# Splitting the first product of chunk 0, sharing the casts of row 1, and letting loads go by VectorE writes

## Chip, cores, metric

One core of a Trainium2 chip. The metric is the device time of one execution in microseconds (us), each kernel run several times. A run counts as slow when it is over 1.5% above the fastest run of the same kernel. That is a label by time alone and says nothing of the cause. Comparisons below use the other runs, called fast; where a median is over all runs, the text says so.

## The reference

Eight rows (batch) of attention with eight heads, 576 positions, head dimension 64. Four heads attend to the last 32 positions, four to every fourth of the last 128. The result, as 4608 tokens of 512 values, goes through a feed-forward layer with a squared relu.

```python
scores = scale * np.matmul(q, k.transpose(0, 1, 3, 2))
mask_plain = (rel >= 0) & (rel < 32)
mask_dil = (rel >= 0) & (rel < 128) & (rel % 4 == 0)
attn = softmax(np.where(masks, scores, -1e9))        # masks by head
x = np.matmul(attn, v).transpose(0, 2, 1, 3).reshape(4608, 512)
h = x @ w_in                 # 512 -> 2048
g = np.maximum(h, 0.0) ** 2
return g @ w_out             # 2048 -> 512
```

## The kernel before

The tokens are cut into nine chunks of 512. TensorE does the *first product* of a chunk (`ph`, with w_in), ScalarE the relu, VectorE the square, TensorE the *second product* (`po`, with w_out). The attention of row b+1 is woven into the products of chunk b. The order of instructions on each engine is the order in which the program writes them: `pump(n)` writes down n steps of the pending product, and what is written between two pumps lands between those steps.

Rows 0 and 1 come through on-chip casts and TensorE transposes. From row 2 on, q and k are copied to DRAM scratch as f16 (`dk`, four copies issued by GpSimd) and transposed by DMA into `QKTx` and `QKTd` (issued by SyncE).

```python
    def store(c, t, po, ots):                 # used by the second product of chunk 0
        ...
        nc.scalar.copy(ot[:, t % 2, :], po)
        if t % 2 == 1:
            rows = out[(c * 4 + t - 1) * P : (c * 4 + t + 1) * P, :]
            nc.gpsimd.dma_start(out=rows.rearrange("(t p) m -> p t m", p=P), in_=ot)

    def keep_qk(b):                           # dk: DRAM to DRAM, f32 to f16
        ...
        for lo in (0, half):
            for i, src in ((1, k), (0, q)):
                nc.gpsimd.dma_start(out=d[i, lo : lo + half], in_=...)
        return d
```

`hold` is a small tile that orders engines: VectorE writes it, then GpSimd does, so GpSimd goes on only once VectorE has come that far.

```python
    ... # row 0: scores and values
    load_sliding_qk(1); load_v(1); load_dilated_qk(1)
    cast_sliding_qk(1, (nc.gpsimd,) * 4)
    load_w_out()
    cast_sliding_v(nc.gpsimd, 2)
    cast_dilated_v(nc.gpsimd, 2)
    g0 = hidden(0)
    pending.append(mm1_gen(0, g0))            # first product of chunk 0
    pump(22)
    begin(1, lambda: pump(1))                 # row 1: transposes and scores
    pump(1000)
    pending.append(mm2_by_rows_gen(0, g0))    # second product; its stores as above
    pump(4)
    ...
    def rows_and_load():
        pump(2)
        n_val[0] += 1
        if n_val[0] == 2:
            nc.vector.memset(hold, 0.0)

    attn_values(1, rows_and_load, True)       # row 1: values
    nc.gpsimd.memset(hold, 0.0)
    dk = keep_qk(2)
    load_v(2)
    transpose_by_dma(dk)
    pump(1000)

    for b in range(2, B):
        pending.append(moe_gen(b - 1))
        ...
        if b == 2:
            ... # GpSimd copies one element of QKTx and QKTd to hold
            dk = keep_qk(b + 1)
            ...
            cast_v(nc.scalar)
            load_v(b + 1)
            pump(4)
        ...
        for g in range(2):
            s_sliding_x(b, g)                 # the scores `ps`, read QKTx
            pump(5)
```

The softmax here doesn't subtract the row's maximum and nothing guards it: scores larger than these inputs give would overflow.

## Time and profile before

| | before |
|---|---|
| time, median of 3 runs | 321.75 us (321.33 to 322.06) |
| span of the profiled run | 318.8 us |
| TensorE busy | 93% |
| mean granted TensorE clock | 0.994 |
| second product of chunk 0 ends (next first product starts) | 67.78 us |
| row 2's q and k transposed (QKTx landed) | 75.34 us |
| first scores of row 2 (ps) | 76.94 us |
| chunks 2 and 3 start | 100.81 and 133.54 us |

Points in time are from the start of the span. (Where the text below gives the end of the second product, it is the start of its last product, 0.2 us earlier: 67.57 here.)

### The profile page before, as it was taken

The page shows a single profiled execution, that of the slowest core. Times are in us where ns is not written, and L with a number is a line of the kernel's source. Part 1 is how long each engine was busy: PE and PEld are TensorE (multiplying, and loading weights), DVE is VectorE, ACT ScalarE, POOL GpSimd, SP SyncE. Part 2 cuts the span into 40 slices and gives each one's busy share as a digit, 9 for nine tenths or more (in the row PEclk, how much of TensorE's full clock was granted, in tenths as well). Part 3 has the DMA queues.
Part 4 walks back from the last instruction along what each step waited for, and adds up shares of the span by engine and source line. Part 5 has one row for each costly group of instructions (what it writes and reads, how often), then busy time and mean ns, then how long its engine had stood idle before and what let it go on. Part 6 is the DMA issues. An engine that isn't in the chain of part 4 may idle for free.

```text
span 318.8 us, 6927 instructions
## 1 busy us (share of the span) xinstructions
PE 295.8 (93%) x2876; PEld 192.5 (60%) x2876; DVE 207.4 (65%) x397; ACT 181.6 (57%) x310; POOL 48.3 (15%) x83
## 2 busy tenths in 40 slices
PE   6768888999998999999999999999999999999992
PEld 2665344544596458845884588458845884684582
DVE  5584486626976597659765976597659765824833
ACT  2754593268934983498349834983498236415620
POOL 4362490213103100120012001200100010000000
PEclk9999997999999999999999999999999999999999
DMA  8999999989998999099939992999220002003003
GB/s 182 236 182 236 209 202 207 238 206 224 211 198 210 204 211 198 23 253 213 191 48 266 201 187 53 251 213 189 53 111 0 2 28 106 0 2 132 2 0 132
DMA packets 82766, 47.88 MB, mean 150 GB/s; under 512 B 67760, under 2 KB 78512, under 8 KB 82352
## 3 DMA queue, kind: packets, MB, share of 16 engines
q1 hardware_dynamic: 74516, 25.99, 42.5%
q0 software_dynamic: 6848, 19.80, 28.0%
q10 hardware_dynamic: 1372, 1.67, 1.9%
q8 instruction: 22, 0.36, 0.5%
q14 instruction: 8, 0.07, 0.1%
HBM read 39.85 MB, written 16.52 MB: 177 GB/s over the span
## 4 chain that ended last, share of the span: by engine, by line
PE 64%; ACT 12%; DMA 11%; DVE 5%; SPq 3%; issue 3%; POOL 1%; ACTq 0%; DVEq 0%; POOLq 0%
PE ph L302 26%; PE poa L350 9%; PE pob L350 8%; PE poc L350 7%; PE pod L350 4%; DMA early<-in_q_dram 3%; ACT vd L145 3%; ACT vp L145 3%; DMA dk<-in_k_dram 3%; DMA QKTx<-dk 2%; DMA sv<-in_v_dram 2%; SPq L106 2%; PE pav L571 2%; PE paw L585 2%; ACT rt L290 2%
## 5 line engine op out<-in xcount | busy, mean ns | idle before, releaser
L302 PE MATMUL ph<-xT,wi 128*128 128x512 f16 x576 | 131.9, 380 | 2.3 <-ACT rt L290 1.7
L290 ACT ACTIVATE rt<-ph 128x512 f16<-128x512 f32 x144 | 83.7, 607 | 23.9 <-PE ph L302 19.7
L302 PEld LDWEIGHTS <-wi 128*128 128x128 f16 x576 | 54.1, 98 | 64.7 <-issue 4.6
L294 DVE TENSOR_TENSOR g<-rt 128x1024 f16<-128x1024 f16 x63 | 44.9, 713 | 50.8 <-ACT rt L290 50.5
L350 PEld LDWEIGHTS <-sm 128*128 128x128 f16 x512 | 47.1, 98 | 7.5 <-issue 2.6
L350 PEld LDWEIGHTS <-g 128*128 128x128 f16 x384 | 35.9, 98 | 6.4 <-DVE g L294 0.3
L350 PE MATMUL poa<-wo,g 128*128 128x256 f16 x256 | 32.8, 273 | 0.1
L350 PE MATMUL pob<-T,sm 128*128 128x256 f16 x256 | 32.5, 272 | 0.0
L606 ACT COPY xT<-px 128x576 f16<-128x576 f16 x16 | 10.2, 640 | 36.9 <-PE px L600 36.9
L366 POOL DMA_DIRECT2D out_dram<-otl x6 | 4.5, 757 | 162.2 <-DVE otl L396 142.8
L624 ACT COPY xT<-py 128x576 f16<-128x576 f16 x16 | 10.2, 638 | 23.0 <-PE py L618 23.0
L554 DVE TENSOR_TENSOR x_d<-paw,rcp_d 72x512 f16<-72x512 f32 x32 | 22.0, 686 | 1.1
L493 DVE TENSOR_TENSOR AT<-AT,maskp 128x576 f16<-128x576 f16 x32 | 16.7, 532 | 7.4 <-ACT AT L492 6.4
L492 ACT ACTIVATE AT<-pz 128x576 f16<-128x576 f32 x32 | 19.3, 680 | 2.6 <-PE pz L539 2.6
L492 ACT ACTIVATE AT<-ps 128x576 f16<-128x576 f32 x32 | 19.3, 664 | 0.4
L553 DVE RECIPROCAL rcp_d<-paw 72x8 f32<-72x8 f32 x32 | 6.5, 203 | 19.5 <-PE paw L585 19.4
L350 PE MATMUL poc<-T,sm 128*128 128x256 f16 x128 | 16.2, 272 | 2.1 <-ACT otu L385 2.1
L554 DVE TENSOR_TENSOR x_p<-pav,rcp_p 96x512 f16<-96x512 f32 x24 | 16.5, 687 | 0.8
L323 PE MATMUL po<-wo,g 128*128 128x512 f16 x64 | 16.9, 399 | 0.0
L350 PE MATMUL poc<-wo,sm 128*128 128x256 f16 x128 | 16.3, 273 | 0.0
L350 PE MATMUL pod<-T,g 128*128 128x256 f16 x128 | 16.1, 273 | 0.0
L493 DVE TENSOR_TENSOR AT<-AT,maskd 128x576 f16<-128x576 f16 x32 | 14.6, 495 | 1.7 <-ACT AT L492 1.5
(89 smaller groups left out, 327.4 us busy)
## 6 DMA issues: line engine op xcount, KB each, us to landing
sv<-in_v_dram SPq DMA_DIRECT2D x40, 128.0 KB, 9.8
sd<-in_v_dram SPq DMA_DIRECT2D x7, 512.0 KB, 6.6
dk<-in_k_dram POOLq DMA_DIRECT2D x12, 288.0 KB, 7.0
dk<-in_q_dram POOLq DMA_DIRECT2D x12, 288.0 KB, 8.7
out_dram<-otl POOLq DMA_DIRECT2D x6, 512.0 KB, 3.4
out_dram<-otu POOLq DMA_DIRECT2D x6, 512.0 KB, 4.3
wi<-in_moe_w_in_dram POOLq DMA_DIRECT2D x2, 1024.0 KB, 11.0
wo<-in_moe_w_out_dram POOLq DMA_DIRECT2D x4, 512.0 KB, 9.7
```

Of the source, the lines that this page charges most:

```text
L145: nc.scalar.copy(o, i)
L290: nc.scalar.activation(rt[:, o, :], ph[:], ACTF.Relu)
L294: nc.vector.tensor_mul(g[:, ffc - 1 : ffc + 1, :], rt, rt)
L302: nc.tensor.matmul(ph, wi[:, dmk, ffc * P : ffc * P + P], xs[:, dmk, :], start=(dmk == 0), stop=(dmk == NDM - 1),)
L323: nc.tensor.matmul(po, g[:, ffc, t * P : (t + 1) * P], wo[:, ffc, :], start=(ffc == 0), stop=(ffc == NFF - 1),)
L350: nc.tensor.matmul(acc[:, t, :], lhs[:, k, t * P : (t + 1) * P], rhs[:, k, :], start=(first and t == 0 and k == 0), stop=(k == NK - 1), sk ...
L492: nc.scalar.activation(AT[:, u, 0:UW], ps[:, :, 0 : UW // 2], ACTF.Exp, scale=scale)
L493: nc.vector.tensor_mul(AT[:, u, 0:UW], AT[:, u, 0:UW], mask)
L553: nc.vector.reciprocal(rcp[0:w], pv[:, :, :, D])
L554: nc.vector.tensor_tensor(out=x[0:w], in0=pv[:, :, :, 0:D], in1=rcp[0:w].unsqueeze(3).to_broadcast([w, 2, HH, D]), op=ALU.mult,)
L606: nc.scalar.copy(xT[:, 0:2, t0 : t0 + 288], px[:, 0:UW].rearrange("x (c t) -> x c t", c=2),)
L624: nc.scalar.copy(xT[:, 2:4, t0 : t0 + 288].rearrange("x c (i r) -> x c i r", r=DIL), py[:, 0:UW].rearrange("x (c r i) -> x c i r", c=2, r= ...
```

## The change

The intent is to start the first product earlier and to take away the waits of row 1. The first 288 tokens of chunk 0 get their own part of the first product, which starts while row 0's last values are still to come. Row 1's q and k casts go from GpSimd to ScalarE and VectorE, its v casts to ScalarE. The w_out load and row 2's v loads are each held until a VectorE write lets them go, so that they keep off the queues of earlier loads.

```diff
+    def mm1_part_gen(c, g, t0, t1):          # first product for tokens t0 to t1
+        ...
-    cast_sliding_v(nc.gpsimd, 2, 0, 2)
+    cast_dilated_v(nc.gpsimd, 2)
     load_w_in()
-    cast_sliding_v(nc.gpsimd, 2, 2, NB)
-    cast_dilated_v(nc.gpsimd, 2)
+    cast_sliding_v(nc.gpsimd, 2)
     ... (row 0; its last values now stand between pumps of the first part)
-    cast_sliding_qk(1, (nc.gpsimd,) * 4)
-    load_w_out()
-    cast_sliding_v(nc.gpsimd, 2)
-    cast_dilated_v(nc.gpsimd, 2)
-    pending.append(mm1_gen(0, g0))
-    pump(22)
-    begin(1, lambda: pump(1))
+    pending.append(mm1_part_gen(0, g0, 0, 288))
+    ...
+    pending.append(mm1_part_gen(0, g0, 288, TOKC))
+    pump(2)
+    nc.vector.memset(hold, 0.0)
+    nc.gpsimd.memset(hold, 0.0)
+    load_w_out()
+    pump(1)
+    cast_sliding_qk(1, (nc.scalar, nc.vector, nc.scalar, nc.vector))
+    pump(2)
+    transposes_and_scores(1, lambda: pump(1))
     pump(1000)
+    cast_v(nc.scalar)
     pending.append(mm2_by_rows_gen(0, g0))
-    pump(4)
+    pump(3)
+    scores_dilated(1, lambda: pump(3))
     ...
         if n_val[0] == 2:
             nc.vector.memset(hold, 0.0)
+            nc.vector.memset(sv[:, :, :, 0:1], 0.0)
+            nc.vector.memset(sd[:, :, :, 0:1], 0.0)
     attn_values(1, rows_and_load, True)
     nc.gpsimd.memset(hold, 0.0)
     dk = keep_qk(2)
     ...
-            pump(4)
+            pump(8)
```

The line `dk = keep_qk(2)` is not touched. But three times `pump(3)` write 9 steps of the second product (two products each) ahead of row 1's values, where `pump(4)` wrote 4. With the 20 steps among the values that makes 29 before `keep_qk(2)`, where there were 24, and a store of chunk 0 belongs to step 28.

More of the change, by code (lines that the diff above doesn't have):

```diff
@@ L294, in relu_squared @@
             nc.vector.tensor_mul(g[:, ffc - 1 : ffc + 1, :], rt, rt)
+    def mm1_part_gen(c, g, t0, t1):
+        xs = xT[:, :, c * TOKC + t0 : c * TOKC + t1]
+        rt = None
+        for ffc in range(NFF):
+            ph = pmool.tile([P, TOKC], FP32, name=f"ph{c}_{ffc}_{t0}", tag="pm")
+            for dmk in range(NDM):
+                nc.tensor.matmul(
+                    ph[:, 0 : t1 - t0],
+                    wi[:, dmk, ffc * P : ffc * P + P],
+                    xs[:, dmk, :],
+                    start=(dmk == 0),
+                    stop=(dmk == NDM - 1),
+                )
+            o = ffc % 2
+            if o == 0:
+                rt = osb.tile([P, 2, TOKC], FP16, name=f"rt{c}_{ffc}_{t0}", tag="rt")
+            nc.scalar.activation(rt[:, o, 0 : t1 - t0], ph[:, 0 : t1 - t0], ACTF.Relu)
+            if o == 1:
+                r = rt[:, :, 0 : t1 - t0]
+                nc.vector.tensor_mul(g[:, ffc - 1 : ffc + 1, t0:t1], r, r)
+            yield
     def mm1_gen(c, g, sm=None):
@@ L627, in x_dilated, with transposes_and_scores @@
         )
-    def begin(b, fill, wide=False):
+    def transposes_and_scores(b, fill):
         for hp in range(2):
             for i in (1, 0):
-                t_sliding(b, hp, i, wide)
+                t_sliding(b, hp, i)
                 fill()
@@ L637, in begin, with scores_dilated @@
             for i in (1, 0):
-                t_dilated(b, g, i, wide, eng=nc.scalar)
+                t_dilated(b, g, i, eng=nc.scalar)
                 fill()
+    def scores_dilated(b, fill):
         for g in range(2):
@@ L663, in attn_values @@
         x_dilated(b, 1, zs, wide)
+    hold = const.tile([P, 1], FP32, name="hold")
     cast_sliding_qk(0, (nc.scalar, nc.scalar, nc.vector, nc.gpsimd))
-    cast_sliding_v(nc.gpsimd, 2, 0, 2)
+    cast_dilated_v(nc.gpsimd, 2)
     load_w_in()
-    cast_sliding_v(nc.gpsimd, 2, 2, NB)
-    cast_dilated_v(nc.gpsimd, 2)
+    cast_sliding_v(nc.gpsimd, 2)
     pj = pmool.tile([P, TOKC], FP32, name="pj", tag="pm")
     idle_matmuls(pj, 14, TOKC)
-    n_idle = [0]
     def idle():
-        n_idle[0] += 1
         idle_matmuls(pj, 5, P)
-    begin(0, idle)
-    def idle_and_load():
-        idle()
-        if n_idle[0] == 15:
-            nc.vector.memset(sq[:, :, :, 0:1], 0.0)
-            nc.vector.memset(nd_[:, :, :, 0:1], 0.0)
-    attn_values(0, idle_and_load)
+    transposes_and_scores(0, idle)
+    scores_dilated(0, idle)
+    xs = [av_sliding(0, 0)]
+    idle()
+    xs.append(av_sliding(0, 1))
+    nc.vector.memset(sq[:, :, :, 0:1], 0.0)
+    nc.vector.memset(nd_[:, :, :, 0:1], 0.0)
+    idle()
+    ys = [av_dilated(0, 0, 0)]
+    idle()
+    x_sliding(0, 0, xs, False)
+    idle()
+    ys.append(av_dilated(0, 0, 1))
+    idle()
+    xs.append(av_sliding(0, 2))
+    idle()
+    x_dilated(0, 0, ys, False)
     load_sliding_qk(1)
@@ L692 @@
     load_dilated_qk(1)
-    cast_sliding_qk(1, (nc.gpsimd,) * 4)
-    load_w_out()
-    cast_sliding_v(nc.gpsimd, 2)
-    cast_dilated_v(nc.gpsimd, 2)
-    g0 = hidden(0)
-    pending.append(mm1_gen(0, g0))
-    pump(22)
-    begin(1, lambda: pump(1))
+    g0 = hidden(0)
+    pending.append(mm1_part_gen(0, g0, 0, 288))
+    zs = []
+    for a in range(2):
+        pump(1)
+        zs.append(av_dilated(0, 1, a))
+    pump(1)
+    x_sliding(0, 1, xs, False)
+    pump(2)
+    x_dilated(0, 1, zs, False)
+    pump(1000)
+    pending.append(mm1_part_gen(0, g0, 288, TOKC))
+    pump(2)
+    nc.vector.memset(hold, 0.0)
+    nc.gpsimd.memset(hold, 0.0)
+    load_w_out()
+    pump(1)
+    cast_sliding_qk(1, (nc.scalar, nc.vector, nc.scalar, nc.vector))
+    pump(2)
+    transposes_and_scores(1, lambda: pump(1))
     pump(1000)
+    cast_v(nc.scalar)
     pending.append(mm2_by_rows_gen(0, g0))
-    pump(4)
+    pump(3)
+    scores_dilated(1, lambda: pump(3))
     n_val = [0]
-    hold = const.tile([P, 1], FP32, name="hold")
     def rows_and_load():
```

## The prediction

> **What bounds the kernel now.** I read the page first. TensorE is busy 93% of 318.8 us, with two soft places: the first 27 us, and the stretch up to about 100 us, where the DMA row never falls below 8 tenths.
>
> ```profile
> PE   6768888999998999999999999999999999999992
> PEclk9999997999999999999999999999999999999999
> DMA  8999999989998999099939992999220002003003
> ```
>
> After that the chunks are TensorE bound: 64 products of 512 columns take 13.81 us in the chain of waits (0.216 us each), and from 105 us on a chunk repeats every 31.85 us. Whatever delays TensorE before 105 us reaches the end one for one. The change touches only that part, so I read the timeline from 14 to 80 us.
>
> ```profile
> 14.83 1.52 POOL L128 DMA_DIRECT2D wi<-in_moe_w_in_dram  x2
> 17.72 3.18 POOL L147 CAST vd<-sd 128x512 f16<-128x512 f32 x4
> ...
> 27.74 9.22 PE L302 MATMUL ph<-xT,wi 128*128 128x512 f16 x42 [0.29 <-ACT xT L624]
> 35.98 3.59 POOL L147 CAST early<-sq 96x768 f16<-96x768 f32 x4 [10.20 <-DMA sq<-in_k_dram]
> ...
> 49.15 0.97 PE L539 MATMUL pz<-QKTd 64*128 64x72 f16 x16 [2.43 <-ACT AT L492]
> 50.05 2.99 PE L323 MATMUL po<-wo,g 128*128 128x512 f16 x8
> ```
>
> Here the reader sees three losses that the change aims at. The first product of chunk 0 runs steadily only from 27.74. It then waits for GpSimd's casts of row 1, whose data landed at 35.98 (the table of stretches gives TensorE 2.07 us of work in 36.9 to 40.4). Then it waits 2.43 us for ScalarE, and the next 8 products run at 0.374 us each, at a lowered clock. Between 27.74 and 67.6, where the second product of chunk 0 ends, I count 34.3 us of TensorE work (13.8 + 13.65 for 64 products each, 6.9 for row 1's attention by the distances in the timeline), so about 5.5 us are lost there.
>
> The next stretch is the one I think decides:
>
> ```profile
> 55.69 0.54 POOL L184 DMA_DIRECT2D dk<-in_k_dram  x1
> ...
> 65.17 6.81 SPq L194 DMA_TRANSPOSE QKTx<-dk  x2
> ...
> 67.14 0.77 POOL L338 DMA_DIRECT2D out_dram<-ot  x1 [9.30 <-ACT ot L335]
> ...
> 67.78 9.23 PE L302 MATMUL ph<-xT,wi 128*128 128x512 f16 x42
> ...
> 75.47 1.03 POOL L730 CAST hold<-QKTx 128x1 f32<-128x1 f16 x1 [5.87 <-DMA QKTx<-dk]
> ...
> 76.94 0.43 PE L520 MATMUL ps<-QKTx 64*128 64x96 f16 x12
> ```
>
> Row 2's q and k are copied to DRAM scratch (dk) from 55.69, then transposed by DMA; the chain of waits has the transposes landing at 75.34, and TensorE asks for them at 76.94. From the first dk issue to the landing are 19.65 us; the slack is 1.6 us. The chain itself runs through dk and QKTx. GpSimd stood 9.30 us at the first store of chunk 0, behind the dk issues.
>
> **What the Trainium skill says.** "TensorE: Matmul & The Clock Gate", Part 1: after an idle window of some 3.4 us the clock is halved until a busy one has passed. This trace agrees: granted clock 0.83 in 46.7 to 50.0, and 0.374 us instead of 0.216 for the products after it. The same page (Engine queue depths) calls ScalarE and VectorE strict FIFO and GpSimd so per core; the 9.30 us at the store fit that. "DMA: Bandwidth & Descriptors", Anatomy of one DMA: DMA engines do not wait on semaphores, the issuing sequencer does; so a store that waits holds what stands behind it on its engine. "ScalarE: Activation LUTs", What ACT_TABLE_LOAD costs: 186 ns plus 0.833 ns per element, some 93 ns overlapped back to back. For 512 columns that gives 613 ns, and the trace has 607.
>
> **The change part by part.**
>
> *Order on GpSimd at the start.* The four casts of vd (3.18 us) now come ahead of the w_in load. The last two need the second sd load, which I put near 15.5 (it took 12.4 us from its issue at 3.11). So they end near 17.2 and w_in is issued 2.3 us later than 14.83. Its halves took 8.1 and 13.9 us to land, at 23.0 and 29.5; now about 25.2 and, with row 1 on the same queues from 22.3, about 32.
>
> *Early start.* From the order of instructions, 288 tokens need only the first halves of both kinds of values. VectorE ends its masks at 20.4, then come normalisations of about 0.87 us each, with two small writes between; the fourth, the last that the first part needs, ends near 24.0, transposes and the copy to xT take 1.2, so the product starts near 25.3 instead of 27.74. It takes over 1.0 us of attention products that earlier ran before it. The part for 288 tokens costs 16 groups of 4 x 0.12 = 7.7 us, but its ninth group needs the second half of w_in: near 30.2 it waits about 2 us. It ends near 36.1. Five groups of 224 tokens (0.4 us each, as weight loads of 98 ns now cover the products) bring TensorE to 38.1.
>
> *Row 1's casts.* Two per engine at 0.83 (ScalarE) and 0.95 us (VectorE), started near 37.6, in place of four on GpSimd at 35.98 to 39.57. The first transposes run near 38.5 instead of 36.85, but with TensorE as far in the product as it was at 40.45. Gain up to here: about 1.5 us.
>
> *ScalarE's stretch.* From 39.2 it has 13 relus of 224 (0.23 us each back to back), two QKTp (0.54), four exponentials (0.54) and eight QKTd (0.29): 8.6 us, to 47.8; then the casts of vp and vd that GpSimd did (1.46 + 1.99 less overlap: 3.3) to 51.1, and only then row 1's dilated exponentials. TensorE does 12 products of the second matrix meanwhile and waits 1 to 2 us for pz. The first sliding values come near 54.0 after 18 products, where before they came at 52.87 after 8, so 55.0 on equal work. The end of the second product moves from 67.6 to about 66.6: **gain 1.0 us**. The lowered clock at 50 us should be gone; it is in that sum.
>
> *Row 2's q and k.* The new pumps (3, 3 and 3, ten times 2) make 29 steps of the second product before row 2's loads are written down, where there were 24. Step 28 issues the first store of chunk 0. The built kernel shows it: on GpSimd the store of ot_0 now stands ahead of the write to hold and the four dk loads. It waits for ScalarE's copy of po_1, and after po_1 TensorE has only 8 products and 8 transposes (2.0 us). So the copy ends about 1.2 us before the second product does, the store issue takes 0.77, and dk starts about 0.2 us ahead of that end, near 66.4, where it was 11.9 us ahead. Row 3 took 78.65 to about 97.7 for the same, row 2 19.65. With v out of the way I take 18.0 us: landed near 84.5.
> TensorE asks for it after 50 products (the pump of 8 moves it from 42): 66.6 + 11.0 = 77.6. **Loss 7.0 us**, standing still.
>
> *After it.* Seven idle microseconds lower the clock; at half rate for some 2.5 us that costs 1.2. ScalarE and VectorE catch up meanwhile (before, 0.5 + 0.2 us of waits at 79 to 81), but the four extra pumps leave row 2's last transposes without products between: about even, +0.0. Rows 3 to 7 have slack enough.
>
> **Sum:** -1.0 + 7.0 + 1.2 = +7.2 on 321.75, so 328.9; I take 328.3, a little down for the catching up of the other engines.
>
> **The rivals.**
> *The intended gain wins (316 to 320):* start 2.4 us earlier, both waits and the lowered clock gone. For it: all three losses are real in the trace. Against it: even with no wait at all the second product cannot end before 25.3 + 34.3 + 1.0 = 60.6; with dk behind the store the scores of row 2 still come near 78.4, after more work done (8 products, 1.7 us), so not faster than before. It needs the store not to hold dk.
> *A wash (321 to 325):* dk and both transposes take only 15 us without v traffic, and the early part gains 3. Against it: no row of this trace took under 19.
> *ScalarE becomes the bound early (330 to 334):* the casts of row 1 and of v stand in its queue ahead of relus, and a late landing stops it. For it: ScalarE was busy 6.06 of 6.30 us in 40.4 to 46.7 and gets 5 us more. Then the second product ends later than before, and everything behind dk with it.
>
> **Range and chances.** The stall has most of the weight: 5.5 to 8.5 us. The early part may lie between -3 and +1.5, the clock between 0.5 and 2. Together 324.5 to 332. The border of 2% is 328.2, next to my figure, so slower and same are nearly equal; faster needs the order on GpSimd to be harmless.
>
> **What would show it.** Right: the ot store ahead of dk on GpSimd with a long wait for ScalarE; dk issued within 1 us of the end of the second product; one TensorE wait of 5.5 to 8.5 us before the ps of row 2 at line 542; a dip in PEclk after it; second product ending 65 to 68. A wait inside the first part near 30 us would show w_in late. Wrong: dk issued near 55 us, ps without a wait, or TensorE past 62 us early.

## The result, and the profile after

The changed kernel takes **332.11 us** (median of 4 runs, 331.3 to 333.33), against 321.54 for four runs of the kernel before. The ratio is 1.0337 with a 95% interval of 1.029 to 1.0384: slower. A ratio here and below is the mean time of one kernel's fast runs over that of the other's in the same rounds, so it is not quite the ratio of the medians quoted.

The rows of the page of the kernel after, in 40 slices of its 329.7 us span, to set beside those of before:

```profile
PE   6887987995699799999999999999999999999992
PEclk9779999999599799999999999999999999999998
DMA  7989995788999999439974995799630003003003
```

The clock's dip at 49 us (7 in the kernel before, 9 here) is missing in this profile. It was not removed for good: of the six other profiles with row 1's v casts on ScalarE, five (e1, e3 to e6) have a dip of 3.4 us that begins between 52.8 and 54.7. A new soft spot stands at 82 us (a 5 and a 6 in the first row), with a halved clock in the second of its slices, and another dip of the clock near 113 us. The longest waits of TensorE in the kernel after, 24 to 112 us (columns: total us, how many, longest):

```profile
PE ps L542 <- DMA QKTx<-dk: 5.6, 1, 5.6
PE pz L561 <- ACT AT L514: 1.8, 2, 1.5
PE ph L302 <- DMA wi<-in_moe_w_in_dram: 1.7, 1, 1.7
PE py L640 <- DVE x_d L576: 1.1, 1, 1.1
PE ph L324 <- ACT rt L290: 1.0, 1, 1.0
```

And the stations of its timeline (start, duration, engine, line, instruction, in brackets the idle time before it and what ended it):

```profile
16.88 1.52 POOL L128 DMA_DIRECT2D wi<-in_moe_w_in_dram  x2
...
32.59 6.01 PE L302 MATMUL ph<-xT,wi 128*128 128x288 f16 x52 [1.70 <-DMA wi<-in_moe_w_in_dram]
...
52.09 2.52 ACT L514 ACTIVATE AT<-pz 128x576 f16<-128x576 f32 x4
...
67.06 0.72 POOL L360 DMA_DIRECT2D out_dram<-ot  x1 [25.67 <-ACT ot L357]
...
67.81 0.53 POOL L184 DMA_DIRECT2D dk<-in_k_dram  x1
...
76.34 6.48 SPq L194 DMA_TRANSPOSE QKTx<-dk  x2
...
85.54 0.67 PE L542 MATMUL ps<-QKTx 64*128 64x96 f16 x12 [5.57 <-DMA QKTx<-dk]
```

GpSimd stands 25.67 us at the first store of chunk 0. The four dk copies are behind it and go out at 67.81, where before they went out at 55.69. Everything that follows is 9 to 12 us later: the transposes are issued at 76.34 against 65.17, the scores of row 2 start at 85.54 against 76.94. And TensorE, with its eight extra products, stands still for 5.57 us before them. Of the list above, the last wait (for ScalarE's `rt`, 0.98 us) lies just before it, and the one at `py` (for VectorE) at the end of row 2.

The wait is paid for twice. Two stretches of the kernel after, by the table of stretches (start:end, length, then busy time and count of TensorE, its weight loads, VectorE, ScalarE and GpSimd, then the granted clock, DMA share and GB/s):

```profile
79.90:86.10 6.20, 0.63 (x13) 0.49 (x12) 3.04 (x5) 0.98 (x3) 0.18 (x1) 0.58 1.06 228
86.10:91.10 5.00, 5.00 (x25) 1.79 (x22) 1.61 (x3) 2.77 (x5) 1.21 (x4) 0.50 0.91 189
```

In the second TensorE is busy all the time, at half clock. The lowered clock lasted from 80.9 to 91.1, so 5.6 us of it after work had begun again, which costs 2.8 us. The ledger at the start of each stretch, after against before, explains the whole:

| stretch | before | after | difference |
|---|---|---|---|
| start to end of second product of chunk 0 | 67.78 | 67.87 | +0.1 |
| from there to ps of row 2 | 9.16 | 17.67 | +8.5, of which 1.7 is 8 more products: +6.8 |
| ps to chunk 2 | 23.87 | 24.92 | +1.05, with 8 products (1.7) fewer: +2.8 |
| chunk 2 to chunk 3 | 32.73 | 33.67 | +0.9 |
| sum | | | +10.6 |

The medians of the four runs each differ by 10.6 as well. (A product costs 0.216 us, from the chain of waits.)

### The profile page after: what moved, and what is told of

Its sections match the earlier page's. It is cut to its first block, busy times and chain, and to the rows that moved or that the text cites. A ratio compares the mean times of both kernels' runs of the same rounds, so it can differ in the third digit from the quotient of the medians.

```text
span 329.7 us, 7031 instructions
## 1 busy us (share of the span) xinstructions
PE 301.4 (91%) x2920; PEld 201.4 (61%) x2920; DVE 208.4 (63%) x409; ACT 188.1 (57%) x331; POOL 39.1 (12%) x73
## 4 chain that ended last, share of the span: by engine, by line
PE 71%; ACT 11%; DMA 10%; DVE 2%; issue 2%; SPq 1%; POOL 1%; ACTq 0%; DVEq 0%
PE ph L324 28%; PE poa L372 9%; PE pob L372 9%; PE poc L372 7%; DMA wi<-in_moe_w_in_dram 5%; PE pod L372 4%; PE po L345 3%; ACT vd L145 3%; ACT vp L145 2%; DMA dk<-in_k_dram 2%; DMA sq<-in_k_dram 2%; PE ph L302 2%; PE paw L607 2%; PE pav L593 2%; PE ps L542 1%
## 5 line engine op out<-in xcount | busy, mean ns | idle before, releaser
L324 PE MATMUL ph<-xT,wi 128*128 128x512 f16 x512 | 119.5, 388 | 1.9 <-ACT rt L290 1.6
L290 ACT ACTIVATE rt<-ph 128x512 f16<-128x512 f32 x128 | 73.8, 602 | 23.5 <-PE ph L324 19.3
L324 PEld LDWEIGHTS <-wi 128*128 128x128 f16 x512 | 49.5, 99 | 61.7 <-issue 8.0
L294 DVE TENSOR_TENSOR g<-rt 128x1024 f16<-128x1024 f16 x56 | 38.7, 691 | 42.4 <-ACT rt L290 42.1
L515 DVE TENSOR_TENSOR AT<-AT,maskp 128x576 f16<-128x576 f16 x32 | 15.9, 503 | 12.0 <-ACT AT L514 10.5
L302 PE MATMUL ph<-xT,wi 128*128 128x288 f16 (+1 forms) x128 | 16.9, 272 | 3.3 <-DMA wi<-in_moe_w_in_dram 1.7
L460 PE MATMUL pj<-zz 128*128 128x128 f16 (+1 forms) x104 | 15.3, 295 | 1.2 <-DVE zz L208 1.2
```

Of the source, the lines that this page charges most:

```text
L290: nc.scalar.activation(rt[:, o, :], ph[:], ACTF.Relu)
L294: nc.vector.tensor_mul(g[:, ffc - 1 : ffc + 1, :], rt, rt)
L302: nc.tensor.matmul(ph[:, 0 : t1 - t0], wi[:, dmk, ffc * P : ffc * P + P], xs[:, dmk, :], start=(dmk == 0), stop=(dmk == NDM - 1),)
L324: nc.tensor.matmul(ph, wi[:, dmk, ffc * P : ffc * P + P], xs[:, dmk, :], start=(dmk == 0), stop=(dmk == NDM - 1),)
L460: nc.tensor.matmul(pj[:, 0:cols], zz[:, 0:P], zz[:, 0:cols], start=True, stop=True)
L515: nc.vector.tensor_mul(AT[:, u, 0:UW], AT[:, u, 0:UW], mask)
```

## The experiments

Twelve kernels ran, all with a correct result. A kernel's runs and those of the kernel before it is compared with come from the same chip; the kernel before had a median of 321.84 us over nine runs there. The first theory was: *the store ahead of dk on GpSimd is the cause; dk sent early brings the time back.* The rivals: *the clock lost after the wait is most of it*; *the changed pump makes TensorE ask too early*; *the later w_in load is what costs*. Diffs are against the kernel after unless said.

| label | what | median, us | ratio to before (95%) |
|---|---|---|---|
| e1_dk_first | dk written ahead of the store | 330.85 | none given |
| e2_warm | TensorE kept busy in the wait | 330.4 | 1.0273 (1.0214 to 1.0332) |
| e3_pump4 | pump(8) back to 4 | 331.68 | 1.032 (1.0255 to 1.0384) |
| e4_wi_first | GpSimd's start order of before | 329.88 | 1.0256 (1.0196 to 1.0317) |
| e5_dk_first_v_free | e1, and v loads not held | 324.6 | 1.0103 (1.0059 to 1.0146) |
| e6_v_free | v loads not held, dk as after | 331.59 | 1.0321 (1.0261 to 1.0381) |
| e7_pool_casts | e5, v casts of row 1 on GpSimd | 321.77 | 0.9985 (0.9929 to 1.0041) |
| e8_all_mends | e7, and e3 and e4 | 320.64 | 0.9927 (0.9843 to 1.0011) |
| e9_stores_late | e8, stores after row 2's transposes | 316.5 | 0.9844 (0.981 to 0.9879) |
| e10_late_8_3_3 | e9, other pumps | 317.18 | 0.9866 (0.9827 to 0.9905) |
| e11_unsplit | e8, first product not split | 318.28 | 0.9869 (0.9807 to 0.993) |
| e12_before_store_first | *before*, store ahead of dk | 330.53 | 1.0278 (1.023 to 1.0327) |

### e1_dk_first: dk ahead of the store

```diff
             nc.vector.memset(sv[:, :, :, 0:1], 0.0)
             nc.vector.memset(sd[:, :, :, 0:1], 0.0)
+            nc.gpsimd.memset(hold, 0.0)
+            dks.append(keep_qk(2))
     attn_values(1, rows_and_load, True)
-    nc.gpsimd.memset(hold, 0.0)
-    dk = keep_qk(2)
+    dk = dks[0]
     load_v(2)
```

> The changed kernel, with the write to hold and the four dk loads of row 2 issued on GpSimd right after the VectorE write at the second sliding value, so ahead of the first store of chunk 0; nothing else moves. My theory (the store in front holds dk, and through it TensorE): dk issued near 57.8 us instead of 67.8, both QKTx landed near 77, TensorE asks near 80 and does not wait; the 5.6 us wait and the lowered clock after it (80.9 to 91.1, about 2.8 us) go, so about 323.5 us against 331.8. Rival (DMA bandwidth: dk would now share the queues with row 2's v, and the transposes land late anyway): a wait of 2 us or more at ps of row 2 stays and the time stays above 327.

Measured: 329.65 and 326.83 us in the two runs called fast, 332.04 and 332.52 in the two called slow. The page was of the 329.65. So the theory, as first stated, failed: dk went out 8.4 us earlier, but no run came near the 323.5 expected, and the wait stayed. The timeline of e1:

```profile
59.39 0.54 POOL L184 DMA_DIRECT2D dk<-in_k_dram  x1
...
67.31 0.69 SPq L113 DMA_DIRECT2D sd<-in_v_dram  x1
...
68.10 1.76 SPq L114 DMA_DIRECT2D sd<-in_v_dram  x1
...
69.96 12.14 SPq L194 DMA_TRANSPOSE QKTx<-dk  x2
...
84.71 0.44 PE L542 MATMUL ps<-QKTx 64*128 64x96 f16 x12 [3.22 <-DMA QKTx<-dk]
```

QKTx landed at 84.58, only 0.8 us earlier than in the kernel after (85.40). The wait is shorter mostly because TensorE asked later: a dip of the clock at 54.7 moved the end of its second product to 69.18. The transposes are issued 10.57 us after dk (8.53 in the kernel after), and the issue of two takes 12.14 us (6.48 there). The v loads of row 2 are let go at 59.2, by the VectorE writes that the change added, in the same instant as dk, so the two share the queues. The last v load is issued at 68.10, and the transposes, which stand behind it on SyncE, 0.1 us after that issue ends. By the trace the third dk copy, which they wait for, had landed at 68.6: some 1.3 us of the delay is SyncE's order. The rest is put down here to the shared queues; no run tested the two apart. Moreover, the queues had just stood nearly idle, as the same stretch shows, first in the kernel before, then in the kernel after (the last two numbers are DMA share and GB/s):

```profile
53.00:57.00 4.00, 4.00 (x46) 2.34 (x44) 2.68 (x7) 0.32 (x1) 1.41 (x4) 1.00 1.24 232
```

```profile
53.00:57.00 4.00, 3.73 (x45) 2.14 (x45) 3.00 (x8) 1.61 (x3) 0.00 (x0) 1.00 0.12 19
```

The second theory: *two holds stand in the way, the store ahead of dk and the writes that hold v; either alone is enough to make row 2 late.*

### e2_warm: TensorE kept busy in the wait

```diff
+        if b == 2 and g == 0:
+            idle_matmuls(tiles[0][:, 0, :], 25, TOKC)   # into the bank that ps overwrites
```

> The changed kernel with 25 idle products of 512 columns into the bank of row 2's first scores, ahead of them, so that TensorE has work (5.4 us) while it waits for QKTx. If the lowered clock after the wait costs what I read, ps stays near 85.5, granted clock stays 1.00 from 80 to 91 us and the time falls by 2.5 to 3 us to about 329. Rival (the clock costs nothing, because the other engines set the pace after the wait, or the wait itself is all): within 0.7 us of the changed kernel.

Measured: 330.4 us. The idle products and a stretch of e2 that answers to the halved one of the kernel after:

```profile
82.24 5.56 PE L460 MATMUL ps<-zz 128*128 128x512 f16 x25
```

```profile
86.00:91.00 5.00, 4.63 (x41) 2.07 (x41) 1.20 (x3) 2.27 (x5) 0.32 (x2) 1.00 1.06 211
```

The clock stayed at 1.00 from 80 to 96 us, and from ps to chunk 2 passed 22.35 us instead of 24.92: 2.57 us less, the size of the 2.8 worked out above. The median gains less (1.7 us on the 332.11 of other rounds; the intervals of the two ratios overlap). The profiled run was the slowest of the four; its second product ended late (70.09, with a dip at 33.6 to 37.0). The clock is a real part of the loss, about a quarter, and not most of it.

### e3_pump4: the pump of 8 back to 4

```diff
-            pump(8)
+            pump(4)
```

> The changed kernel with the 4 steps of before in place of 8 ahead of row 2's scores. TensorE asks for QKTx 1.7 us earlier and waits that much longer (7.3 us), at the same 85.5; the work it did before now comes after, so that alone is 0. At the end of row 2 there are products between the last transposes again: the 1.1 us wait for VectorE there and the second lowered clock (111.6 to 115.0) go, so 1.5 to 2.5 us less, about 330. Rival (the tail of row 2 does not matter, 8 steps help): 331.8 or up to 1.7 us more.

Measured: 331.68 us, with a wait of 7.7 us before ps. TensorE asks earlier by 8 products and waits longer by about as much; ps starts at 85.9 all the same. The landing of QKTx sets that start, and the pump is not the cause of the wait. What was expected for the end of row 2 did come in the profile: the wait at `py` is shorter, and the second dip of the clock is gone. The wait and the clock row of e3:

```profile
PE py L640 <- DVE x_d L576: 0.6, 1, 0.6
```

```profile
PEclk9599997999599999999999999999999999999998
```

From chunk 2 to chunk 3 pass 32.73 us, as in the kernel before, against 33.67 in the kernel after. The median shows little of this: it is 0.4 us lower, the runs spread over 2.9 us, and in the profiled one a dip at 52.8 made the second product end 1.1 us later.

### e4_wi_first: GpSimd's start order of before

```diff
-    cast_dilated_v(nc.gpsimd, 2)
+    cast_sliding_v(nc.gpsimd, 2, 0, 2)
     load_w_in()
-    cast_sliding_v(nc.gpsimd, 2)
+    cast_sliding_v(nc.gpsimd, 2, 2, NB)
+    cast_dilated_v(nc.gpsimd, 2)
```

> The changed kernel with GpSimd's start in the order of before: first vp cast, then the w_in load, then the others. w_in is issued near 14.8 instead of 16.9, its second half lands near 30 instead of 32.5, the 1.7 us wait of the first part goes, and row 1's k lands near 36 instead of 37.8; the second product of chunk 0 ends 1 to 2 us earlier and the rest follows: about 330.3. Rival (ScalarE with the casts of v bounds this part, so data that come earlier buy nothing): within 0.6 us of the changed kernel.

Measured: 329.88 us, by its verdict unclear. The early part gained: row 1's first transpose at 37.19 instead of 38.99, the second product started at 46.46 instead of 48.27. But by its end the 1.8 us were gone (68.24, after a wait of 2.3 us for ScalarE and a dip at 52.9 to 56.3), and the wait before ps was 5.7 us. So the lead was lost to ScalarE and the clock before the store, and the store's wait stayed. The median lies 2.2 us under the 332.11 of other rounds, with overlapping intervals: whether w_in first gains anything by itself is not shown.

### e6_v_free and e5_dk_first_v_free: the second theory

e6 takes the two writes that hold v out, and leaves dk behind the store:

```diff
-            nc.vector.memset(sv[:, :, :, 0:1], 0.0)
-            nc.vector.memset(sd[:, :, :, 0:1], 0.0)
```

> The changed kernel without the two VectorE writes to sv and sd, dk still behind the store: the other half of e5. In the changed kernel v had landed (67.55) before dk began to move, so v earlier gives nothing here by itself: dk near 67.8, QKTx near 85, wait of 5 to 6 us, time within 1.5 us of the changed kernel (330 to 332.5). Rival (v's late start is the whole loss): 326 or less.

Measured: 331.59 us. v goes early, dk still waits behind the store (69.44), and TensorE waits as before:

```profile
86.79 0.67 PE L542 MATMUL ps<-QKTx 64*128 64x96 f16 x12 [5.20 <-DMA QKTx<-dk]
```

e5 does both: e6's edit and e1's.

> As e1 (dk ahead of the store), and the two VectorE writes to sv and sd are left out, so that row 2's v is let go by the casts of row 1's v (near 51 to 52) and not at 57.7. After e1 my first theory (the store alone) has fallen: dk came 8.4 us earlier, but shared the queues with v, and the second QKTx landed at 84.58 all the same. New theory: row 2's v, dk, transposes and stores are one stretch of DMA work that must not begin at 57.7, and dk must not be last in it. Then here v lands by 61 as before the change, dk lands by 67 to 69, QKTx by 78 to 79, and TensorE, which asks near 80, waits under 1 us; no lowered clock near 85; 322 to 325 us. Rival 1 (store alone, e1 spoilt by chance): as e1, 327 to 331. Rival 2 (the transposes are slow whatever comes before them): QKTx past 82, above 327.

Measured: **324.6 us** (324.36 to 325.81), some 7 us less than e6 in the same rounds. The timeline of e5:

```profile
58.89 0.54 POOL L184 DMA_DIRECT2D dk<-in_k_dram  x1
...
66.43 6.57 SPq L194 DMA_TRANSPOSE QKTx<-dk  x2
...
80.85 0.43 PE L542 MATMUL ps<-QKTx 64*128 64x96 f16 x12
```

dk goes out at the same time as in e1 (58.89 against 59.39). But v has landed by 61.1, the transposes take 6.57 us to issue instead of 12.14, QKTx lands at 76.2, and ps has no wait. This is what the two edits do singly and together, in time and in the landing of QKTx: neither 332.1 us and 85.40; v alone 331.6 and 86.65; dk alone 326.8 to 332.5 and 84.58; both 324.6 and 76.20. By the landings the second theory holds. By the times dk alone may bring back a part: its two faster runs lie 2.5 and 5.3 us under 332.1.

### e12_before_store_first: the store's place alone, in the kernel before

The reverse test: the kernel *before*, with one line that changes nothing in the order of TensorE, VectorE or SyncE, only on GpSimd.

```diff
     attn_values(1, rows_and_load, True)
+    pump(4)
     nc.gpsimd.memset(hold, 0.0)
     dk = keep_qk(2)
```

> The kernel before, with four steps more of the second product written ahead of row 2's loads: by the order of instructions TensorE, VectorE and SyncE stay the same, and on GpSimd the first store of chunk 0 stands ahead of the write to hold and the four dk loads. If the store ahead of dk makes the loss by itself when v is early, then dk near 67.9 instead of 55.7, QKTx near 85.5, TensorE asks at 77 and waits about 8 us, a lowered clock after it, and 330 to 333 us. Rival (the loss of the change needs its other parts, above all the new work on ScalarE): under 326.

Measured: 330.53 us, slower by 2.8%. The timeline of e12:

```profile
66.80 0.72 POOL L338 DMA_DIRECT2D out_dram<-ot  x1 [20.31 <-ACT ot L335]
...
67.55 0.53 POOL L184 DMA_DIRECT2D dk<-in_k_dram  x1
...
77.04 5.58 SPq L194 DMA_TRANSPOSE QKTx<-dk  x2
...
85.26 0.66 PE L520 MATMUL ps<-QKTx 64*128 64x96 f16 x12 [8.58 <-DMA QKTx<-dk]
```

With neither split, nor casts moved, nor v held, one store written ahead of four copies costs 8.7 us (330.53 less 321.84). This is the mechanism the prediction named, shown by itself.

### e7_pool_casts, e8_all_mends: the other parts put right

e7 is e5 with row 1's v casts on GpSimd again; e8 adds the edits of e3 and e4.

```diff
-    cast_v(nc.scalar)
+    cast_sliding_v(nc.gpsimd, 2)
+    cast_dilated_v(nc.gpsimd, 2)
     pending.append(mm2_by_rows_gen(0, g0))
```

> As e5, and row 1's v is cast on GpSimd, as before the change, in place of ScalarE. The 1.5 to 2.9 us that TensorE waits at pz for ScalarE (casts of vp and vd stand ahead of the exponentials) go, and with them the lowered clock in the second product of chunk 0; its end comes 2 to 3 us earlier (near 65.5). If QKTx then lands in time, 319.5 to 322; if it is now QKTx that TensorE waits for, the gain is eaten and the time is that of e5. Rival (ScalarE was not what held pz): end of the second product as in e5.

> As e7, with GpSimd's start in the order of before (w_in first) and 4 steps ahead of row 2's scores: what is left of the change is the split first product with its early start, and row 1's q and k cast on ScalarE and VectorE. If the idea of the change is sound and only its order of loads and casts was not, the second product ends near 64 and the time is 317 to 320, below the kernel before. If DMA sets the pace of this whole stretch, TensorE waits for QKTx instead and it is 320.5 to 323, the kernel before again.

Measured: e7 321.77 us over all six runs, two of them slow (330.5 and 336.02); ratio of the fast ones 0.9985. The wait for ScalarE before the dilated scores' exponentials is gone, and the second product ends at 67.28 instead of e5's 68.61, in spite of a dip. The intervals of e5's and e7's ratios do not overlap: the v casts on ScalarE were a cost. None of the profiles of e7 to e11 has the dip at 53 to 58 us. e8: 320.64 us, in two groups (316.6 twice, 320.3 to 321.3 four times). Its second product ends at 63.88, the gain that the change was meant to have, but in the profiled run, one of the second group, a wait is back:

```profile
64.42 10.17 SPq L194 DMA_TRANSPOSE QKTx<-dk  x2
...
77.25 0.44 PE L542 MATMUL ps<-QKTx 64*128 64x96 f16 x12 [3.93 <-DMA QKTx<-dk]
```

The transposes' issue takes 10.17 us here. The two stores of chunk 0 (512 KB each) now go out at 63.29 and 65.18, beside them.

### e9_stores_late: the stores after the transposes

```diff
-            nc.gpsimd.dma_start(out=rows.rearrange("(t p) m -> p t m", p=P), in_=ot)
+            late.append((rows.rearrange("(t p) m -> p t m", p=P), ot))
     ...                                # at b == 2, after GpSimd's copies to hold:
+            for o, i in late:
+                nc.gpsimd.dma_start(out=o, in_=i)
             dk = keep_qk(b + 1)
```

> As e8, with both stores of chunk 0 issued after the transposes of row 2 have landed. In e8 TensorE waits 3.9 us for QKTx (77.1), and the two stores move beside the transposes (63.3 to 74.5). If DMA bandwidth is what holds QKTx, it lands near 74.5, the wait falls to 1 to 2 us, 318 to 319.5. Rival (the transposes go at their own pace): QKTx near 77, time as e8 (320).

Measured: **316.5 us** (316.14 to 317.01, six runs), ratio 0.9844: the fastest kernel, 1.6% under before. The timeline of e9:

```profile
62.03 6.84 SPq L194 DMA_TRANSPOSE QKTx<-dk  x2
...
73.30 0.43 PE L544 MATMUL ps<-QKTx 64*128 64x96 f16 x12
...
76.90 1.51 POOL L783 DMA_DIRECT2D out_dram<-ot  x2
```

QKTx lands at 71.36, ps starts at 73.30 without a wait, and chunk 2 at 97.19, where before it was 100.81. The clock row of its page has 9 in every slice from 24 us to the last but one. The two stores have nobody who waits for them.

### e10_late_8_3_3 and e11_unsplit: is there more, and what is the split worth

e10 is e9 with `pump(8)` and with `pump(3)` after each sliding score of row 2:

```diff
-            pump(4)
+            pump(8)
     ...
-            pump(5)
+            pump(3 if b == 2 else 5)
```

> As e9, with 8 steps ahead of row 2's scores as in the change, and 3 in place of 5 after each of the two sliding scores, so that row 2's transposes keep products between them. TensorE asks 1.7 us later: no wait if QKTx lands near 75; 317 to 318.5, and no lowered clock. Rival (ScalarE and VectorE fall behind with the scores closer together): as e9 or more.

Measured: 317.18 us, not faster than e9 (its interval of ratios overlaps e9's).

e11 is e8 with the first product of chunk 0 in one part again, after row 0's attention:

```diff
-    pending.append(mm1_part_gen(0, g0, 0, 288))
-    ... (row 0's last values between pumps)
-    pending.append(mm1_part_gen(0, g0, 288, TOKC))
-    pump(2)
+    ... (row 0's last values between idle products)
+    pending.append(mm1_gen(0, g0))
+    pump(18)
```

> As e8, but the first product of chunk 0 in one piece after row 0's attention, as before the change: what the early start of 288 tokens is worth. If it is worth its 1.7 to 2 us at TensorE, the second product ends near 66 instead of 63.9. But e8 then waits for QKTx at 77.1 anyway, so the time moves less than that: 320 to 322. Rival (the early start is worth nothing, the gain of e8 came from the casts): end near 64, time as e8.

Measured: 318.28 us over all six runs, two of them slow; ratio of the fast ones 0.9869, against e8's 0.9927 with overlapping intervals. The profile fell into a slow run (TensorE waited 5.18 us for QKTx there, beside the two stores, as in e8), so its times after about 70 us are left aside. Before that, row 1's first transpose (37.09 against e8's 37.24) and the end of the second product (63.19 against 63.88) come no later than with the split. So the split, the visible heart of the change, shows no gain here: TensorE starts earlier, and what it wins has been given back by the first transpose of row 1.

## Why the prediction was right and wrong

**The direction and the mechanism were right.** The built order showed the store ahead of dk on GpSimd; the prediction had dk issued near 66.4, it came at 67.81; QKTx landing near 84.5, it landed at 85.4; one long wait at line 542 of 5.5 to 8.5 us, it was 5.57; a dip of the clock after it, it came; second product ending between 65 and 68, it ended at 67.65. The 7.0 us of "standing still" measured 6.8 (5.57 in the wait at ps and 0.98 in one for ScalarE just before). The median, 332.11, lies just above the range that was given, 324.5 to 332.0. What failed are the two terms around this wait, both mis-sized to the same side: the gain ahead of it, and above all what comes after it.

**"Gain 1.0 us" at the end of the second product: measured a loss of 0.1.** The parts came nearly as worked out: first product begun at 25.13 (said 25.3), w_in issued at 16.88 (said about 17.1) and its second half awaited for 1.70 us (said about 2), row 1's transposes at 38.99 (said 38.5). The step that failed is ScalarE's stretch: it began at 39.57 (said 39.2), stood idle for 0.37 us and took 0.3 us longer than reckoned, so its casts of v ended at 52.1, not 51.1, and the first sliding values came at 55.12, not 54.0. Before, they came at 52.87 with ten products fewer done, 55.03 on equal work. So by that point all of the lead had been given back. The rival in which ScalarE becomes the bound early was thus partly true, and e7, which takes those casts off it, bears that out. And this profile was lucky. In five others with the same early part (e1, e2, e3, e5, e6) the second product ends between 68.6 and 70.1; each of them has a dip of the clock between 24 us and that point, this one has none.

**"Half rate for some 2.5 us that costs 1.2", and "+0.0" for what comes after: measured 2.8 and 0.9 in the ledger.** This is the larger miss. The clock was low for 5.6 us of work, not 2.5; e2 put that at 2.57 us by taking it away. And the four extra pumps, of which the prediction said that they leave row 2's last transposes without products, were not "about even". At the end of row 2 TensorE waited 0.69 and 1.13 us for VectorE, where before it waited 0.55, and from 111.6 to 115.0 the clock was low once more. That dip goes with the pump: every profile with pump(8) and the old pumps behind it (after, e1, e2, e4 to e7) has one there and takes 33.3 to 33.7 us from chunk 2 to chunk 3; every other (before, e3, e8 to e12) has none and takes 32.73. Together these terms are 3.7 us where 1.2 was said.

**The sum.** Predicted -1.0 + 7.0 + 1.2 = +7.2, and then taken down a little to 6.6 "for the catching up of the other engines". Measured +0.1 + 6.8 + 3.7 = +10.6. The reduction leaned on two waits of 0.5 and 0.2 us in the kernel before. These did go, but the new waits at the end of row 2 took more. In e12, which keeps the pump of 4, ps to chunk 2 takes 24.37 us against 23.87 before, though the clock was low for 4.3 us of it, which at half rate costs 2.2: there most of the lost clock was made up. (One reading was loose: chunks repeat every 31.85 us from chunk 3 on, 133.54, and not from 105 us.)

**What the prediction did not see.** It took "18.0 us with v out of the way" from dk to landing, as though v were out of the way whenever dk comes late. In the kernel after that is so (17.6 us). But it did not see that the writes holding v make a second hold, ready to cost nearly as much once the first is mended; only e1 and e5 showed it. And the wash that it put against the mechanism ("dk and both transposes take only 15 us") was refused because no row of the trace took under 19; e5 and e9 took 17.3 and 17.2, so for row 2 that refusal was right.

**What stays open.** Runs of one kernel differ by several us (e1 by 5.7; e8's two groups, 316.6 and 320.3 to 321.3), in e7 by 16. The place of the clock's dips changes from profile to profile and may be behind this, but no experiment controlled it, and only one run of each kernel has a profile. And e9's gain over before is the sum of several parts (dk about 1.5 us earlier, the early writes, casts on ScalarE and VectorE, late stores) that were not tried one by one; only the split was, and it shows none.

## What to carry to other kernels

Where a store waits for a late result, look at what is written behind it on the same issuing engine: a transfer that the next stage needs must be issued ahead of it, and a change of a few pump counts can turn the two around without a line about them in the diff. When one hold is mended, check that a second one (here a gate on loads that share the queues) doesn't stand at the same place, before you drop the theory. And reckon a long wait at its length plus what the lowered clock costs afterwards (2.57 us by e2), less what is made up later (most of it in e12).

## What the Trainium skill lacked or had wrong

- "TensorE: Matmul & The Clock Gate", Part 1, gives an idle window of about 3.4 us as what lowers the clock, and about 3.4 us of sustained work as what restores it. The halving to 0.50 and the steps of 3.4 us agree with every dip here. What it does not give is how much work still counts as idle: the clock fell although TensorE had been busy for 1.22 (before, to 48.9), 1.48 (after, to 80.9) and 1.83 us (e5, to 104.4) of the 3.40 us up to then. So the prediction's "this trace agrees" is right for the halving, but not for the idle window: the longest gap before 48.9 was 2.43 us. In the kernel after, 2.16 busy us of the 3.40 from 84.3 did not restore the clock; 3.40 of 3.40, to 91.1, did.
- "DMA: Bandwidth & Descriptors", Latency and other measured facts, gives a DMA transpose with a non-contiguous middle dimension 261 GB/s, and a contiguous one more. Here two of 128 x 2304 f16 values (0.59 MB each) for row 2, issued one after the other, took 7.1 us from the first issue to the last landing at best (e10), 167 GB/s, and 14.6 us (81 GB/s) with v loads and two stores on the queues (e1). That table gives no figure for a transpose beside other transfers; here the two took twice as long.
- No page that I read gives a time for copies from DRAM to DRAM with a cast. Of four of 288 KB written (dk, row 2), the third, for which the transposes wait, landed 7.5 us (e5) to 10.5 us (e10) after the first issue.
